# Another bilinear scheme for the first layer of a top-1 expert, with the sums of the second layer's weights on another engine

## The chip, the cores and the metric

The kernel runs on one core of a Trainium2 chip. The metric is the device time of one execution in microseconds (us). The engines are named as in the profile: PE is the matrix engine (PEld its weight loads), DVE, ACT and POOL the vector, scalar and GpSimd engines, SP the one that issues most transfers.

## The reference

An attention block feeds a mixture of experts. Everything is fp32.

```python
def _attn_ref(q, k, v, alpha):                       # 4 x 8 heads, 768 steps, 48 wide
    for t in range(S):
        state = alpha[:, :, t, :, None] * state + np.einsum('bhd,bhe->bhde', k[:, :, t], v[:, :, t])
        y[:, :, t] = np.einsum('bhd,bhde->bhe', q[:, :, t], state)
    ...
def _moe_ref(x, expert_emb, tau, w1, w2):            # x 3072 x 384; 8 experts; w1 384 x 1024, w2 1024 x 384
    xn = x / (np.linalg.norm(x, axis=-1, keepdims=True) + 1e-06)
    ...
    expert_idx = np.argmax(logits, axis=1)
    ...
    gate_w = probs[np.arange(N), expert_idx]
    for e in range(E):
        mask = expert_idx == e
        h = np.maximum(x[mask] @ w1[e], 0.0)
        out[mask] = gate_w[mask, None] * (h @ w2[e])
```

Each of the 3,072 rows goes to one expert, about 384 rows to each; a row's result is its gate times `relu(x w1) w2`.

## The kernel before

From 0 to about 162 us of the profile the kernel computes the attention and the router, and writes the rows to HBM sorted by expert. The rest of the time is the mixture of experts. An expert's rows are taken as three whole blocks of 128 rows, plus a half block of 64 rows that runs only for experts with more than 384 rows. Expert 0 is computed in the plain way (`first_layer`, `second_layer`), two of its blocks early; experts 1 to 7 run as follows (`run(i)`), and the change concerns these.

**First layer** (`first_layer_blocks`). The transposed rows `xT` (384 x 384) and `w1` (384 x 1024) are cut in blocks: `w1` into 2 x 3 blocks of 128 x 512 (`halves_w1`), the rows into 3 x 3 blocks of 128 x 128. The product is made by a bilinear scheme of 15 block products in place of 18. Sums of weight blocks are in `w1_m` (ten of 128x512), sums of row blocks in `xT_m` (16 of 128x128). One product is 4 matmuls of 128 columns each. [...]`bank(j)` names one of four in pool `ps_q` (tiles `pq`), and pools `ps_y` (tiles `pyo`) and `ps_x` (tiles `pxg`) have two each. Several products accumulate in one bank and are read out between two of them; the part read is copied (ACT) or added (DVE) into a block of the hidden rows `hT`, and `relu` runs in place on ACT. A product into a bank waits for the last reader of that bank. The chains start in banks 2, 1, 0 and 3:

```python
            A, B, C, D = (grid(j) for j in (2, 1, 3, 0))
```

**Second layer.** The third block goes through `second_layer` (16 rows in the profile, 128x384). The first two go through `second_layer_pair`, seven products of 2 x 2 blocks, each 4 matmuls of 192 columns, in banks 0, 1 and 3:

```python
            a, b, d = (bank(j)[:, 0:m] for j in (0, 1, 3))
            ...
            product(a, a22, t4, False, True)
            done_pair[:] = pe[0], by_act(nc.scalar.mul, y1[:, 0:m], a, g1)
            done_pair.append(scatter(y1, col[:, 1:2]))
```

Its sums of hidden blocks `s1` to `s4` come from `mix_hidden` (DVE, 128x512), its sums of `w2` blocks `t1` to `t4` from `mix_weights` (DVE, 128x768). The results `y` are scattered to their rows by POOL (`scatter`).

**What sets the order.** PE's products are kept in written order by `pe_turn`: each is issued after the one before. `by_dve` and `by_act` do the same for the DVE and ACT work that they carry. What carries none of these is placed by a scheduler from dependences. `between` transposes a block of the next expert's rows on PE and copies it to `xT` on ACT; `squares` takes the squared norm of a block of its rows on ACT; `norm`, `begin_gates` and `gates_end` make its gates. The sums of the next expert's `w1` blocks (`mix_first_weights`) run on POOL, those of its row blocks (`mix_first_rows`) on DVE beside the second layer. For expert 1 the `w1` sums are on DVE. Weights have three buffers (`NW`), loaded by SP two experts ahead.

**The half block** (`run_extra`) stands behind a branch on a value loaded at run time. In the program it comes after the first matmuls of the next expert's first layer, and every engine passes the branch. It ran for experts 0, 3 and 4.

Of the kernel before, what the change touches and what calls it, by code (L numbers as in the profile page):

```python
# [9 lines left out]
FP32 = mybir.dt.float32  # L10
I32 = mybir.dt.int32
AF = mybir.ActivationFunctionType
# [15 lines left out]
def kernel(  # L28
# [797 lines left out]
    with ExitStack() as c3:  # L826
# [12 lines left out]
        w2_m = wp.tile([P, 4, FT // 2, DM // 2], FP32, name="w2_m")  # L839
        hT_m = xp.tile([P, 4, FT // 2, P], FP32, name="hT_m")  # L840

        w1_m = wp.tile([P, 10, F // 2], FP32, name="w1_m")
        xT_m = xp.tile([P, 16, P], FP32, name="xT_m")
        NG = 3
        gt_s = [xp.tile([P, NC + 1], FP32, name=f"gt{i}") for i in range(NG)]
        sx_s = [xp.tile([P, NC + 1], I32, name=f"sx{i}") for i in range(NG)]
# [139 lines left out]
        def by_dve(call, *args, **kwargs):  # L986
            with turn_of(dve):
                dve[:] = [call(*args, **kwargs)]  # L988
            return dve[0]

        def by_act(call, *args, **kwargs):
            with turn_of(act):
                act[:] = [call(*args, **kwargs)]  # L993
            return act[0]
# [5 lines left out]
            n, m = FT // 2, DM // 2  # L1000
            return [[w2_t[:, i * n : i * n + n, j * m : j * m + m] for j in range(2)] for i in range(2)]

        def mix_weights(w2_t):

            (b11, b12), (b21, b22) = quarters(w2_t)
            t1, t2, t3, t4 = (w2_m[:, k] for k in range(4))
            for to, x, y in ((t1, b12, b11), (t2, b22, t1), (t3, b22, b12), (t4, b21, t2)):
                by_dve(nc.vector.tensor_tensor, to, x, y, ALU.subtract)

        def hidden(hT, t):  # L1010

            return [hT[:, j * FT // 2 : (j + 1) * FT // 2, t * P : (t + 1) * P] for j in range(2)]
# [9 lines left out]
            by_dve(v.tensor_tensor, s2, s1, a11, ALU.subtract)  # L1022
            by_dve(v.tensor_tensor, s4, a12, s2, ALU.subtract)

        def halves_w1(w1_t):

            return [[w1_t[:, k, j * F // 2 : (j + 1) * F // 2] for k in range(KT)] for j in range(2)]

        def mix_first_weights(i, by):

            (a11, a12, a13), (a21, a22, a23) = halves_w1(w1_s[i % NW])
            g, g2, e, f2, q9, q7, q10, k6, q13, k = (w1_m[:, j] for j in range(10))
            for to, x, y, op in (
                (g, a11, a12, ALU.add), (g2, g, a22, ALU.subtract), (e, a12, a13, ALU.subtract),
                (f2, e, a22, ALU.subtract), (q9, a21, g2, ALU.subtract),
                (q7, a23, q9, ALU.subtract), (q10, g, q7, ALU.subtract),
                (k, f2, a23, ALU.add), (k6, k, a21, ALU.subtract),
                (q13, q7, a13, ALU.subtract),
            ):
                by(to, x, y, op)  # L1040

        def mix_first_rows(i):

            xT, m = xT_s[i % 2], xT_m
            b1, b2, b3 = (xT[:, k, 0 : NC * P].rearrange("p (t n) -> p t n", n=P) for k in range(KT))
            y1, z1, y2, z2, x5, x12, x10, x6, x1, x4, x7, x13, s, x15, x11, x14 = (
                m[:, j : j + 1] for j in range(16)
            )
            v = nc.vector

            def one(b, t):
                return b[:, t : t + 1]

            v.tensor_tensor(m[:, 0:2], b2[:, 1:3], b3[:, 1:3], ALU.add)
            v.tensor_tensor(y2, one(b2, 0), one(b1, 0), ALU.subtract)
            v.tensor_tensor(x1, y1, y2, ALU.add)
            v.tensor_tensor(x11, y2, one(b3, 0), ALU.add)
            v.tensor_tensor(m[:, 4:6], b1[:, 0:2], y1.to_broadcast([P, 2, P]), ALU.subtract)
            v.scalar_tensor_tensor(
                out=x4, in0=y2, scalar=-1.0, in1=one(b3, 1), op0=ALU.mult, op1=ALU.subtract  # L1060
            )
            v.tensor_tensor(x7, z1, one(b1, 0), ALU.subtract)
            v.tensor_tensor(s, one(b2, 2), one(b3, 1), ALU.add)
            v.tensor_tensor(m[:, 6:8], s.to_broadcast([P, 2, P]), b1[:, 0:3:2], ALU.subtract)
            v.tensor_tensor(x13, one(b1, 2), z1, ALU.subtract)
            v.tensor_tensor(z2, one(b1, 2), one(b2, 2), ALU.subtract)
            v.tensor_tensor(x14, one(b3, 0), x7, ALU.subtract)
            v.tensor_tensor(x15, one(b1, 1), x6, ALU.add)

        def first_layer_blocks(w1_t, hT, between, squares):  # L1070

            (a11, a12, a13), (a21, a22, a23) = halves_w1(w1_t)
            g, g2, e, f2, q9, q7, q10, k6, q13, k = (w1_m[:, j] for j in range(10))
            y1, z1, y2, z2, x5, x12, x10, x6, x1, x4, x7, x13, _, x15, x11, x14 = (
                xT_m[:, j] for j in range(16)
            )
            (c11, c21), (c12, c22), (c13, c23) = (hidden(hT, t) for t in range(NC))
            n = FT // 2

            def grid(j):  # L1080
                return bank(j)[:, 0 : n * P].rearrange("p (f t) -> p f t", t=P)

            A, B, C, D = (grid(j) for j in (2, 1, 3, 0))

            def product(to, left, right, start, stop):
                with pe_turn():
                    for f in range(n):
                        pe[:] = [nc.tensor.matmul(  # L1088
                            to[:, f], lhsT=left[:, f * P : (f + 1) * P], rhs=right,
                            start=start and f == 0, stop=stop, skip_group_check=True,  # L1090
                        )]

            def add(c, p):
                by_dve(nc.vector.tensor_tensor, c, p, c, ALU.add)

            def relu(c, p):
                return by_act(nc.scalar.activation, c, p, AF.Relu)

            product(A, a22, x1, True, False)
            by_act(nc.scalar.copy, c21, A)  # L1100
            product(B, g2, y1, True, False)
            by_act(nc.scalar.copy, c12, B)
            product(D, a13, x11, True, True)
            by_act(nc.scalar.copy, c11, D)
            between()
            squares()
            product(A, f2, y2, False, False)
            add(c11, A)
            product(B, g, x5, False, False)
            add(c11, B)  # L1110
            relu(c11, c11)
            D = grid(0)
            product(D, a11, x12, True, True)
            add(c12, D)
            between()
            product(A, e, x4, False, False)
            add(c12, A)
            relu(c12, c12)
            squares()
            product(B, q7, x7, False, False)  # L1120
            by_act(nc.scalar.copy, c13, B)
            product(C, q10, x10, True, False)
            by_act(nc.scalar.copy, c23, C)
            between()
            squares()
            squares()
            product(A, k6, x6, False, False)
            add(c13, A)
            product(B, q9, z1, False, False)
            add(c23, B)  # L1130
            product(C, q13, x13, False, True)
            add(c13, C)
            relu(c13, c13)
            product(A, k, z2, False, False)
            add(c23, A)
            relu(c23, c23)
            product(B, a23, x14, False, True)
            add(c21, B)
            relu(c21, c21)
            between()  # L1140
            product(A, a21, x15, False, True)
            return relu(c22, A)

        def second_layer_pair(w2_t, hT, gate, col):

# [74 lines left out]
        def run(i):  # L1220
# [6 lines left out]
            pair = blocks_run(i) == NC  # L1227
            dve[:] = [] if pair else ready
            if pair:
                mix_weights(w2_t)  # L1230
                left, late = list(range(len(nxt))), list(range(len(nxt)))
                if nxt:
                    known = begin_gates(i + 1, by_dve)

                def between():
                    if left:
                        prepare(i + 1, left.pop(0), lambda *args: by_act(nc.scalar.copy, *args))

# [8 lines left out]
                first_layer_blocks(w1_t, hT, between, squares)  # L1247
# [143 lines left out]
```

## Time and profile before

| | us |
|---|---|
| time, median of 3 runs | 408.04 (407.83 to 408.78) |
| the profiled execution's own time | 416.09 |
| its span (first to last instruction) | 414.2 |
| mean granted clock of PE, as a share of full speed | 0.988 |
| mixture of experts | about 162 to 410 of the span |
| one expert (the one that ends at 365.84) | 29.39 |
| of it: first layer; third block's second layer; pair's second layer | 15.09; 5.16; 9.14 |

The profile is of one execution, which was slower than the median of the runs. Its page gives busy time of each engine, the span in slices, and groups of instructions as "line engine op, output<-input, partitions x elements, count | busy us, mean ns of one | idle time before and what ended it". One fp32 matmul of the program shows as two rows of the matrix engine.

### The profile page before, as it was taken

Reading aid. Unit: us, or ns where it says so; the run is one execution under the profiler, and the core shown is the slowest. Engines: PE = TensorE matmul, PEld = TensorE weight load, DVE = VectorE, ACT = ScalarE, POOL = GpSimd, SP = SyncE. Lnnn points to the kernel's source line nnn. Section 1 sums busy time; section 2 is a strip of 40 time slices with the busy share of each in tenths; the row PEclk is TensorE's granted clock in tenths of the full one; section 3 lists DMA queues with packets and bytes.
Section 4 is the critical chain, followed back from the end, with each engine's and each line's share of the span. In section 5 each row is a group of like instructions: output and inputs, shape, how many; then the busy total and the mean of one; then the engine's idle time right before and its main releaser. Section 6 shows DMA issues by size and latency. Waiting matters only on the chain. (4 is left out here: it accounts for less than half of the span.)

```text
span 414.2 us, 12556 instructions
## 1 busy us (share of the span) xinstructions
PE 396.5 (96%) x4954; PEld 353.6 (85%) x4954; DVE 282.9 (68%) x638; ACT 195.2 (47%) x481; POOL 220.8 (53%) x284
## 2 busy tenths in 40 slices
PE   6999999999999789999999999999999999999994
PEld 6889989898899567679989989899979979979974
DVE  7878979698989216872696695691594389397530
ACT  4455545455555324463653734823651572662320
POOL 7455677776666336721853834822761581682001
PEclk8999999999999899999999999999999999999998
DMA  9999999999987892695604706505601900101001
GB/s 137 158 165 154 152 193 181 193 174 189 206 180 172 283 359 102 183 350 181 220 18 160 254 18 223 183 19 183 227 19 41 358 9 19 40 2 41 15 16 44
DMA packets 119379, 60.28 MB, mean 146 GB/s; under 512 B 102287, under 2 KB 113816, under 8 KB 119312
## 3 DMA queue, kind: packets, MB, share of 16 engines
q1 hardware_dynamic: 115208, 49.14, 49.6%
q0 software_dynamic: 3728, 10.16, 6.8%
q8 instruction: 46, 0.75, 0.8%
q14 instruction: 21, 0.17, 0.1%
q10 hardware_dynamic: 376, 0.05, 0.1%
HBM read 49.69 MB, written 11.45 MB: 148 GB/s over the span
## 5 line engine op out<-in xcount | busy, mean ns | idle before, releaser
L858 POOL DMA_INDIRECT out_dram<-y,sx x25 | 24.6, 983 | 102.8 <-DVE y L1167 42.3
L988 DVE TENSOR_TENSOR hT<-pq,hT 128x512 f32<-128x512 f32 x63 | 43.4, 691 | 46.4 <-PE pq L1088 41.9
L1088 PE MATMUL pq<-xT_m,w_m 128*128 128x128 f32 x560 | 67.2, 275 | 0.0
L1088 PEld LDWEIGHTS pq<-xT_m,w_m 128*128 128x128 f32 x560 | 64.8, 192 | 0.3 <-issue 0.3
L512 POOL TENSOR_TENSOR qs<-qc,a 128x512 f32<-128x512 f32 x24 | 30.6, 1275 | 33.5 <-DVE a L508 17.6
L1040 POOL TENSOR_TENSOR w_m<-w_m,w 128x512 f32<-128x512 f32 x30 | 43.2, 1447 | 1.4
L971 PE MATMUL pyo<-w,hT 128*128 128x384 f32 x128 | 42.6, 486 | 0.0
L1088 PE MATMUL pq<-xT_m,w 128*128 128x128 f32 x280 | 38.4, 277 | 0.6
L993 ACT ACTIVATE hT<-hT 128x512 f32<-128x512 f32 x35 | 22.1, 631 | 31.2 <-DVE hT L988 31.2
L1088 PEld LDWEIGHTS pq<-xT_m,w 128*128 128x128 f32 x280 | 34.9, 192 | 2.1 <-issue 1.8
L971 PEld LDWEIGHTS pyo<-w,hT 128*128 128x128 f32 x128 | 23.7, 190 | 14.8
L479 DVE TENSOR_TENSOR_SCAN r<-pa,inr 128x511 f32<-128x511 f32 x24 | 29.2, 1217 | 7.0 <-PE pa L194 4.6
L191 PE MATMUL sc<-qs,kr 64*64 64x128 f32 x768 | 29.3, 273 | 4.5 <-issue 4.5
L311 POOL DMA_INDIRECT xs<-x,dest x24 | 24.2, 1009 | 14.4 <-DVE x L655 9.4
L508 DVE TENSOR_TENSOR_SCAN a<-pa,ini 128x512 f32<-128x512 f32 x24 | 29.3, 1222 | 1.1
L1160 PE MATMUL pq<-w_m,hT_m 128*128 128x192 f32 x168 | 28.4, 326 | 0.0
L191 PEld LDWEIGHTS sc<-qs,kr 64*64 64x64 f32 x768 | 22.3, 133 | 7.0 <-issue 6.5
L1160 PEld LDWEIGHTS pq<-w_m,hT_m 128*128 128x128 f32 x168 | 27.5, 190 | 0.0
L191 PE MATMUL pyx<-sm,vt 128*64 128x128 f32 x384 | 26.3, 279 | 0.0
L191 PEld LDWEIGHTS pyx<-sm,vt 128*64 128x64 f32 x384 | 20.5, 136 | 4.1 <-issue 3.4
L1040 POOL TENSOR_TENSOR w_m<-w 128x512 f32<-128x512 f32 x12 | 15.3, 1276 | 15.9 <-PE pq L1088 15.9
L651 ACT COPY lg<-pyx 128x32 f32<-128x32 f32 x24 | 4.4, 185 | 41.0 <-PE px L191 35.1
(229 smaller groups left out, 910.3 us busy)
## 6 DMA issues: line engine op xcount, KB each, us to landing
w<-in_moe_w_dram SPq DMA_DIRECT2D x16, 1536.0 KB
kt<-in_k_dram SPq DMA_DIRECT2D x24, 192.0 KB
qt<-in_q_dram SPq DMA_DIRECT2D x24, 192.0 KB
vt<-in_v_dram SPq DMA_DIRECT2D x24, 192.0 KB
xg<-xs SPq DMA_DIRECT2D x22, 196.5 KB
at<-in_alpha_dram SPq DMA_DIRECT2D x24, 168.0 KB
xg<-xs SPq DMA_DIRECT2D x8, 98.2 KB
at<-in_alpha_dram SPq DMA_DIRECT2D x24, 22.5 KB
```

The source lines that it names most:

```text
L191: last["pe"] = nc.tensor.matmul(*args, **kwargs)
L311: ins = nc.gpsimd.indirect_dma_start(out=xs, out_offset=bass.IndirectOffsetOnAxis(ap=rows, axis=0), in_=x, in_offset=None, bounds_check=E ...
L479: nc.vector.tensor_tensor_scan(r[:, L - 2 :: -1], pa[:, L - 1 : 0 : -1], inr[:, L - 2 :: -1], 1.0, ALU.mult, ALU.add,)
L508: d["a_scan"] = by_dve = nc.vector.tensor_tensor_scan(a, pa, ini, 0.0, ALU.mult, ALU.add)
L512: by_pool = nc.gpsimd.tensor_tensor(qs.rearrange("p n t -> p (n t)"), d["qc"], a, ALU.mult)
L858: ins = nc.gpsimd.indirect_dma_start(out=out, out_offset=bass.IndirectOffsetOnAxis(ap=col, axis=0), in_=y, in_offset=None, bounds_check=N - 1,
L971: pe[:] = [nc.tensor.matmul(py, lhsT=hT[:, f], rhs=w2_t[:, f], start=(f == 0), stop=(f == FT - 1),)]
L988: dve[:] = [call(*args, **kwargs)]
L993: act[:] = [call(*args, **kwargs)]
L1040: by(to, x, y, op)
L1088: pe[:] = [nc.tensor.matmul(to[:, f], lhsT=left[:, f * P : (f + 1) * P], rhs=right, start=start and f == 0, stop=stop, skip_group_check=Tr ...
L1160: pe[:] = [nc.tensor.matmul(to, lhsT=left[:, f], rhs=right[:, f], start=start and f == 0, stop=stop and f == n - 1, skip_group_check=True,)]
```

## The change

The first layer is cut in another way: `w1` into 3 x 4 blocks of 128 x 256 (`columns_w1`), the rows into 3 x 2 blocks of 128 x 192 (`rows_x`). The scheme has 20 block products in place of the 24 of that cut. One product is 2 matmuls of 192 columns. There are 16 sums of weight blocks (128x256) and 13 of row blocks (128x192). The chains are in banks 0, 1, 2 and 3, two further chains follow in banks 0 and 2, and two products stand `alone` in `ps_y`. The first four products take row blocks as they are, without sums. The sums of `w2` blocks are issued on POOL for experts 2 to 7 and stay on DVE for expert 1.

```diff
-        w1_m = wp.tile([P, 10, F // 2], FP32, name="w1_m")
-        xT_m = xp.tile([P, 16, P], FP32, name="xT_m")
+        TH, FQ = NC * P // 2, F // 4
+        w1_m = wp.tile([P, 16, FQ], FP32, name="w1_m")
+        xT_m = xp.tile([P, 13, TH], FP32, name="xT_m")
...
-        def mix_weights(w2_t):
+        def mix_weights(w2_t, by):
...
-                by_dve(nc.vector.tensor_tensor, to, x, y, ALU.subtract)
+                by(to, x, y, ALU.subtract)
...
+        def columns_w1(w1_t):
+            return [w1_t[:, k, j * FQ : (j + 1) * FQ] for k in range(KT) for j in range(4)]
+        def rows_x(xT):
+            return [xT[:, k, t * TH : (t + 1) * TH] for t in range(2) for k in range(KT)]
...
         def mix_first_weights(i, by):
...
+            w = columns_w1(w1_s[i % NW]) + [sum_w1(j) for j in range(12, 28)]
             for to, x, y, op in (
+                (14, 8, 9, ALU.add), (16, 4, 6, ALU.add), (20, 0, 8, ALU.add),
...
+                by(w[to], w[x], w[y], op)
...
+        def first_layer_blocks(w1_t, xT, hT, between, squares):
...
+            c = [hT[:, 2 * j : 2 * j + 2, t * TH : (t + 1) * TH] for t in range(2) for j in range(4)]
...
+            def alone():
+                return grid(ps_y.tile([P, DM], FP32, name="pyo"))
             def product(to, left, right, start, stop):
                 with pe_turn():
-                    for f in range(n):
+                    for f in range(2):
                         pe[:] = [nc.tensor.matmul(
-                            to[:, f], lhsT=left[:, f * P : (f + 1) * P], rhs=right,
+                            to[:, f], lhsT=w[left][:, f * P : (f + 1) * P], rhs=x[right],
...
-            def add(c, p):
-                by_dve(nc.vector.tensor_tensor, c, p, c, ALU.add)
+            def add(j, p, op=ALU.add):
+                by_dve(nc.vector.tensor_tensor, c[j], c[j], p, op)
...
+            A, G, D, B = (chain(j) for j in (0, 1, 2, 3))
+            product(A, 11, 5, True, False)
+            put(7, A)
+            product(G, 4, 4, True, False)
+            put(4, G)
+            product(D, 20, 5, True, False)
+            add(4, D)
+            product(B, 15, 4, True, False)
+            add(7, B, ALU.subtract)
             between()
+            product(A, 13, 9, False, False)
+            put(6, A, -1.0)
...
+            E3 = chain(0)
+            product(E3, 27, 0, True, False)
+            add(1, E3, ALU.subtract)
+            relu(1)
...
+            y = alone()
+            product(y, 0, 15, True, True)
+            add(4, y)
+            relu(4)
             squares()
...
+            X4 = chain(2)
+            product(X4, 23, 18, True, False)
+            add(2, X4, ALU.subtract)
+            relu(2)
             squares()
+            product(E3, 1, 10, False, True)
+            add(5, E3)
+            relu(5)
+            product(B, 25, 16, False, True)
+            add(3, B)
+            relu(3)
+            product(X4, 22, 6, False, True)
+            add(0, X4)
+            relu(0)
             squares()
             squares()
...
-                mix_weights(w2_t)
+                if i == 1:
+                    mix_weights(w2_t, lambda *args: by_dve(nc.vector.tensor_tensor, *args))
+                else:
+                    mix_weights(w2_t, nc.gpsimd.tensor_tensor)
```

`chain(j)` is `bank(j)` seen as two halves of 192 columns; `put` copies a bank into a block of `hT` on ACT, with a sign; `grid` before gave four parts of 128 columns.

More of the change, by code (lines that the diff above doesn't have):

```diff
@@ L1023, in mix_hidden, with sum_w1, sum_x @@
             by_dve(v.tensor_tensor, s4, a12, s2, ALU.subtract)
-        def halves_w1(w1_t):
-            return [[w1_t[:, k, j * F // 2 : (j + 1) * F // 2] for k in range(KT)] for j in range(2)]
+        def columns_w1(w1_t):
+            return [w1_t[:, k, j * FQ : (j + 1) * FQ] for k in range(KT) for j in range(4)]
+        def rows_x(xT):
+            return [xT[:, k, t * TH : (t + 1) * TH] for t in range(2) for k in range(KT)]
+        def sum_w1(j):
+            return w1_m[:, j - 12]
+        def sum_x(j):
+            return xT_m[:, j - 6]
@@ L1029, in mix_first_weights @@
         def mix_first_weights(i, by):
-            (a11, a12, a13), (a21, a22, a23) = halves_w1(w1_s[i % NW])
-            g, g2, e, f2, q9, q7, q10, k6, q13, k = (w1_m[:, j] for j in range(10))
+            w = columns_w1(w1_s[i % NW]) + [sum_w1(j) for j in range(12, 28)]
             for to, x, y, op in (
[L1034 to L1038, printed above, removed]
+                (14, 8, 9, ALU.add), (16, 4, 6, ALU.add), (20, 0, 8, ALU.add),
+                (15, 3, 7, ALU.subtract), (12, 2, 10, ALU.add), (13, 11, 12, ALU.add),
+                (17, 2, 16, ALU.subtract), (19, 0, 14, ALU.add), (18, 5, 15, ALU.add),
+                (21, 16, 13, ALU.subtract), (24, 5, 13, ALU.subtract), (26, 1, 19, ALU.add),
+                (27, 18, 26, ALU.subtract), (23, 2, 6, ALU.subtract), (25, 7, 24, ALU.subtract),
+                (22, 17, 14, ALU.subtract),
@@ L1039, in mix_first_weights @@
             ):
-                by(to, x, y, op)
+                by(w[to], w[x], w[y], op)
         def mix_first_rows(i):
[L1044 to L1083, printed above, removed]
+            xT, v = xT_s[i % 2], nc.vector
@@ new lines, in mix_first_rows, with minus_sum @@
+            x = rows_x(xT) + [sum_x(j) for j in range(6, 19)]
+            def minus_sum(to, a, b):
+                v.scalar_tensor_tensor(
+                    out=x[to], in0=x[a], scalar=-1.0, in1=x[b], op0=ALU.mult, op1=ALU.subtract
+                )
+            for to, a, b, op in (
+                (8, 3, 4, ALU.add), (6, 0, 2, ALU.subtract), (7, 1, 6, ALU.add),
+                (9, 7, 5, ALU.subtract), (11, 4, 7, ALU.add),
+            ):
+                v.tensor_tensor(x[to], x[a], x[b], op)
@@ new lines, in mix_first_rows, with grid, chain @@
+            minus_sum(13, 0, 5)
+            for to, a, b, op in (
+                (12, 0, 4, ALU.subtract), (14, 2, 5, ALU.add), (18, 1, 4, ALU.add),
+            ):
+                v.tensor_tensor(x[to], x[a], x[b], op)
+            minus_sum(17, 8, 9)
+            for to, a, b, op in (
+                (15, 3, 5, ALU.subtract), (10, 0, 3, ALU.add), (16, 0, 1, ALU.add),
+            ):
+                v.tensor_tensor(x[to], x[a], x[b], op)
+        def first_layer_blocks(w1_t, xT, hT, between, squares):
+            w = columns_w1(w1_t) + [sum_w1(j) for j in range(12, 28)]
+            x = rows_x(xT) + [sum_x(j) for j in range(6, 19)]
+            c = [hT[:, 2 * j : 2 * j + 2, t * TH : (t + 1) * TH] for t in range(2) for j in range(4)]
+            def grid(whole):
+                return whole[:, 0 : 2 * TH].rearrange("p (f t) -> p f t", t=TH)
+            def chain(j):
+                return grid(bank(j))
+            def alone():
+                return grid(ps_y.tile([P, DM], FP32, name="pyo"))
@@ L1096, in relu @@
[L1096 to L1104, printed above, removed]
-            between()
-            squares()
-            product(A, f2, y2, False, False)
-            add(c11, A)
-            product(B, g, x5, False, False)
@@ L1110, in first_layer_blocks, with put, relu @@
[L1110 to L1114, printed above, removed]
+            def put(j, p, sign=1.0):
+                if sign > 0:
+                    by_act(nc.scalar.copy, c[j], p)
+                else:
+                    by_act(nc.scalar.mul, c[j], p, -1.0)
+            def add(j, p, op=ALU.add):
+                by_dve(nc.vector.tensor_tensor, c[j], c[j], p, op)
+            def relu(j):
+                by_act(nc.scalar.activation, c[j], c[j], AF.Relu)
@@ new lines, in first_layer_blocks @@
+            A, G, D, B = (chain(j) for j in (0, 1, 2, 3))
[7 more added lines that the diff above has]
+            add(7, B, ALU.subtract)
+            between()
+            product(A, 13, 9, False, False)
+            put(6, A, -1.0)
+            product(G, 17, 11, False, False)
+            put(0, G, -1.0)
@@ new lines, in first_layer_blocks @@
+            product(D, 19, 13, False, False)
+            put(5, D, -1.0)
+            product(B, 18, 12, False, False)
+            add(5, B, ALU.subtract)
+            between()
+            product(A, 12, 14, False, True)
+            put(3, A, -1.0)
+            put(2, A)
+            product(G, 21, 7, False, False)
+            add(2, G)
+            product(D, 9, 14, False, True)
+            put(1, D)
+            add(0, D, ALU.subtract)
+            product(B, 5, 18, False, False)
+            add(1, B)
@@ new lines, in first_layer_blocks @@
+            between()
+            E3 = chain(0)
+            product(E3, 27, 0, True, False)
+            add(1, E3, ALU.subtract)
+            relu(1)
+            product(G, 2, 17, False, True)
+            add(6, G, ALU.subtract)
+            relu(6)
+            y = alone()
+            product(y, 0, 15, True, True)
+            add(4, y)
+            relu(4)
+            squares()
+            y = alone()
+            product(y, 3, 8, True, True)
+            add(7, y)
+            relu(7)
@@ L1115, in first_layer_blocks @@
             between()
-            product(A, e, x4, False, False)
-            add(c12, A)
-            relu(c12, c12)
+            X4 = chain(2)
+            product(X4, 23, 18, True, False)
+            add(2, X4, ALU.subtract)
+            relu(2)
             squares()
[L1120 to L1124, printed above, removed]
+            product(E3, 1, 10, False, True)
@@ L1125, in first_layer_blocks @@
+            add(5, E3)
[6 more added lines that the diff above has]
+            relu(0)
             squares()
             squares()
[L1127 to L1142, printed above, removed]
         def second_layer_pair(w2_t, hT, gate, col):
@@ L1229, in run @@
             if pair:
-                mix_weights(w2_t)
+                if i == 1:
+                    mix_weights(w2_t, lambda *args: by_dve(nc.vector.tensor_tensor, *args))
+                else:
+                    mix_weights(w2_t, nc.gpsimd.tensor_tensor)
                 left, late = list(range(len(nxt))), list(range(len(nxt)))
@@ L1245, in norm @@
                         gates_norm(known, len(nxt), by_dve, by_act)
-                first_layer_blocks(w1_t, hT, between, squares)
+                first_layer_blocks(w1_t, xT, hT, between, squares)
                 mix_hidden(hT, norm)
```

## The prediction

> **What bounds the kernel now.** I read the page's engine totals first, then its slices, then the window of one expert, then the timeline around the place where one expert's products end and the next one's begin.
>
> ```profile
> PE 396.5 (96%) x4954; PEld 353.6 (85%) x4954; DVE 282.9 (68%) x638; ACT 195.2 (47%) x481; POOL 220.8 (53%) x284
> PE   6999999999999789999999999999999999999994
> 350.75:365.84 15.09, 14.94 (x134) 14.78 (x133) 8.11 (x16) 9.23 (x22) 10.49 (x9) 1.00 0.08 29
> 336.45:365.84 29.39, 29.24 (x206) 26.90 (x205) 21.39 (x45) 15.10 (x33) 16.48 (x14) 1.00 0.06 21
> ```
>
> PE is busy 96% of the span. In the last two lines (start:end, length, busy time of PE, PEld, DVE, ACT and POOL, granted clock) one first layer takes 15.09 us and a whole expert 29.39 us, and PE lacks 0.15 us in each. So DVE's 21.4 and POOL's 16.5 us per expert cost nothing while they come in time: a change counts here by columns streamed through PE and by waits put into PE's queue.
>
> ```profile
> 341.61 2.76 PE L1160 MATMUL pq<-w,hT 128*128 128x192 f32 x16
> 344.21 4.06 PE L1160 MATMUL pq<-w_m,hT_m 128*128 128x192 f32 x24
> 349.41 1.50 PE L1160 MATMUL pq<-w_m,hT 128*128 128x192 f32 x8
> 350.59 0.80 PEld L1088 LDWEIGHTS pq<-xT_m,w 128*128 128x128 f32 x6
> 350.75 1.44 PE L1088 MATMUL pq<-xT_m,w 128*128 128x128 f32 x8
> 350.95 0.42 ACT L993 ACTIVATE y<-pq,gt 128x192 f32<-128x192 f32 x1 [3.52 <-PE pq L1160]
> 351.70 0.30 PEld L1088 LDWEIGHTS pq<-xT_m,w 128*128 128x128 f32 x2 [0.31 <-issue]
> ```
>
> This is the timeline (start, duration, engine, line, operation, count, idle time before it). The second layer's last product begins at 349.41 and its last matmul at 350.59; the next expert's first layer follows at 350.75 without a gap. ACT empties that last product's bank only from 350.95 to 351.37, beside the new products. The only idle PE time is 0.31 us at 351.70, where the instructions ahead of the half-block branch drain.
>
> **What the Trainium skill says.** (1) "TensorE: Matmul & The Clock Gate", § Back-to-back issue gap, gives N/2.4 + 2.5 ns for an isolated warm matmul. With the columns counted twice, my fit for fp32, that is 109.2 ns at 128, 162.5 at 192 and 322.5 at 384. The trace, start to start: 111.7, 162.5 (24 in 3.90 us, 344.21 to 348.11) and 322.6. It agrees at 192 and 384, and 128 costs 2.5 ns more. (2) "PSUM — Partial Sum Buffer", § PSUM bank collisions raise a hardware error, says that the hardware does not arbitrate two engines in one bank, so software must guard by bank. The trace shows the cost of such a guard nowhere at this boundary, since the next product uses another bank. (3) "SBUF — State Buffer", § Who interferes with whom: a DVE instruction with two SBUF inputs contends with a GpSimd instruction that reads SBUF, one with at most one SBUF input does not. The trace agrees: adds of PSUM and SBUF take 691 ns beside POOL's sums, sums of two SBUF operands of that size 680 to 690 alone and 1290 to 1490 beside POOL. (4) "GPSIMD Engine Reference", § 4.1 Engine selection, puts two-input work at about twice DVE's time on GpSimd; here 128x512 takes 1276 on POOL and 680 on DVE.
>
> **The products.** Each fp32 matmul is two rows here. A first layer was 15 products x 4 x 2 = 120 rows of 128 columns; it becomes 20 x 2 x 2 = 80 rows of 192. The streamed columns are the same, 120 x 128 = 80 x 192 = 15,360. Time: 120 x 0.1117 = 13.40 us before, 80 x 0.1625 = 13.00 after, **-0.40 us** for each of seven first layers, all on the path. The four groups of three transposes (0.327 us each) and the branch's drain stay: 13.40 + 1.31 + 0.38 = 15.09, as measured.
>
> **The new wait.** The second layer's pair uses banks 0, 1, 3; its last product (`a22`, `t4`) is in bank 0 and is read by `y1[:, 0:m]` on ACT. Before, the first layer started in bank 2 (`A`), which the pair never touches. Now `A` is bank 0, so its first LDWEIGHTS waits for that ACT instruction, and everything on PE is behind it: the branch, 19 products, the transposes. Priced from the rows: the last matmul at 350.59 is released to ACT at 350.95; ACT takes 0.42, to 351.37; from an evacuation's end to the LDWEIGHTS it frees is 0.06 (DVE ends 188.61, PEld 188.67), the matmul 0.03 later. That is 351.46 instead of 350.75, 0.71 us, and about 0.04 for the cold restart of the weight load: **+0.75 us**. Bounds: 0.42, ACT's own time, if the handovers cost nothing (less than 0 is excluded, since a wait only adds), and 0.95 if the branch is lengthened too. PE's branch loads a value and compares it; by the trace's records that ended at 350.23, beside the last product and 1.4 us ahead of the drain. Now both are queued behind the wait and end 0.9 us after it; the two or three matmuls ahead of the branch drain at 0.9 as well, so I take 0. It happens before six first layers (experts 2 to 7). Expert 1's first layer follows no pair, so has no such wait; before it there is a wait for x and the half block in any case, and DVE's w1 sums for it cost PE some 0.15: I count -0.25 there.
>
> Sum: 6 x (-0.40 + 0.75) - 0.25 = **+1.85 us**. The profiled execution, 416.09 us (414.2 span and 1.9 around it), would become 417.9; the median of 408.04, 2% under that execution, 409.9.
>
> **Inside the first layer.** Sums left in PSUM are now read 14 times by DVE (before 9) and copied 8 times by ACT (before 5), each 128x384. A line through DVE's 128x256 (about 400 ns) and 128x512 (691) gives 0.55 us: 7.7 us of 14.3. ACT: 8 copies at 0.48 (128x384 has that row), 8 relus at about 0.53 (from 631 at 512), 4 copies of xT and 4 squares with their accumulator reads (0.48, 0.73) come to 12.9 of 14.3, though overlapped issue leaves less. A product into a bank waits for its last reader. Walking all 20 with 0.20 us from product end to reader, the tightest is the last one (`X4`, bank 2): it wants `add(2, X4)` at 13.13 and would start at 13.67. At least 0.5 us is spare everywhere, so I cost this at 0; the cover is the three products in other banks between two uses of one. The second layer needs the last relus by 0.8 us less than I find. The squares moved to the end make `s2` on DVE ready about 6 us after the second layer starts; its product needs it at 7.76.
>
> **Sums of x** (13 of 128x192, cadence about 0.27 = 3.5 us, before 3.1) are needed only from the fifth product on, since the first four take x itself. They end some 0.7 us later, ahead of the pair's DVE evacuations, the last of which that PE waits for comes 2 us later: 0. **Sums of w1** on POOL: 16 of 128x256 at 613 ns (row L537) = 9.8 us, before ten at 1276 to 1447 = 13.6. **Sums of w2**, four of 128x768: DVE's 0.956 x 4 = 3.8 us per expert go, but PE waited for none of them, so nothing is gained. On POOL each is 1276 x 768/512 = 1.9 us (estimate), 7.7 in all; per expert POOL then has 9.8 + 7.7 + 3 scatters of 0.98 = 20.5 of 29.4 us. Expert 1's stay on DVE. POOL's queue has them ahead of the pair's scatters (`t1` to `t3` before `y0`, `t4` before `y1`), so these leave 2.4 and 3.4 to 5 us later; the three y buffers are wanted 20 us later, so 0. The w1 sums follow at 7 to 17 us into the first layer (before from 5.4); they are needed in the next one: 0. SP's transfers are the same in number; an expert's weights are issued about 1 us later and are used more than 30 us later: 0. The tail after the last pair does not change.
>
> **Rivals.**
>
> A. *The wait on bank 0 costs nothing* (faster): ACT's emptying is met by something PE waited for anyway. For it: nothing in the profile; against it: PE has no gap at 350.75. Then 7 x -0.40 + 0.15 = -2.65, 405.4 us. It decides the sign at a wait of 0.44 us a boundary; between 0.30 and 0.58 the result is within 0.8 us of no change, which is 0.2%, about what a measurement of this kernel can tell from no change.
>
> B. *The evacuations fall behind* (slower than my forecast): 30 PSUM and relu steps in 13 us, in an order by hand, on ACT above all. It decides when an add or a copy with its handover exceeds the 0.65 us of a product for several in a row. Each first layer then loses 0.3 to 1 us more: +2 to +7, 412 to 417 us. Against it: the 0.5 us of slack.
>
> C. *DVE's adds meet POOL's sums on the shared port*: the operand order is now SBUF first, PSUM second. If ten adds rise from 0.55 to 1.1 us, a first layer loses 3 to 4 us once the slack is used: from 431 on. Against it: 691 ns beside POOL with the same two memories.
>
> D. *The move to POOL does what it is for but not for PE*: DVE has 3.8 us more room in 29.4 and PE, which never waited for those sums, gains 0. This is inside my forecast; were PE to wait for `t3` or `t4` on POOL, 1.9 us x 6 would be lost, 421. `t4` is done over 20 us before its product.
>
> **How the numbers follow.** Forecast with the wait at 0.6 to 0.95: 0.70, 409 to 411.1. Wait only partly felt: 0.10, 408.0 to 408.8. A: 0.07. B: 0.09. C and a late POOL: 0.04. So faster 0.07, same 0.10, slower 0.83. The range 408.0 to 413.5 leaves out A, C and the upper half of B, some 0.16.
>
> **What would show it.** Right: at the boundary PEld idle some 0.7 us before the first layer's first LDWEIGHTS, released by ACT y; a first layer of 14.7 us from its first matmul (80 rows at 162.5); an expert of 29.74 instead of 29.39; DVE's busy time about 10 us less (6 x 3.8, less 7 x 1.5 for more adds and some for the sums of x); POOL rows of 128x768 near 1.9 us. Wrong: no idle time there (A); idle time inside the first layer with DVE or ACT hT as releaser (B); adds of 128x384 over 0.9 us (C); a pair's product released by POOL (D).

## The result, and the profile after

The changed kernel takes 422.03 us (median of 6 runs, 419.93 to 423.66), the kernel before 408.56 in the same comparison: a ratio of **1.0301** (95% interval 1.0265 to 1.0336), slower. The forecast was 409.9 with a range of 408.0 to 413.5. The profiled execution took 420.01 us, with a span of 418.2.

The spans (414.2 and 418.2) are no measure here: the profiled execution of before came some 8 us later to the experts, by a slower stage ahead of them. I compare the stretch from the start of expert 1's pair to the start of expert 7's: 211.80 to 399.25 before, **187.45 us**, and 204.21 to 403.26 after, **199.06 us**: 11.6 more.

First the page's totals, its slices of PE and of the granted clock, then four windows of the changed kernel: a pair, the first layer after it (expert 2), and those of experts 3 and 6.

```profile
PE 393.4 (94%) x4674; PEld 348.5 (83%) x4674; DVE 257.6 (62%) x655; ACT 206.0 (49%) x516; POOL 252.0 (60%) x344
PE   7899999989999899999999969999999996999994
PEclk9999999999999999999999998999999998899999
```

```profile
204.21:213.98 9.77, 9.26 (x57) 8.96 (x55) 5.88 (x21) 2.56 (x7) 5.23 (x4) 1.00 0.05 17
213.98:228.79 14.81, 14.66 (x92) 14.31 (x93) 6.56 (x12) 9.04 (x22) 14.13 (x18) 1.00 0.80 287
244.87:264.11 19.24, 16.34 (x93) 15.92 (x94) 7.01 (x13) 9.05 (x22) 15.08 (x18) 0.91 0.64 218
349.26:369.68 20.42, 17.21 (x93) 16.79 (x93) 7.01 (x13) 9.05 (x22) 13.81 (x17) 0.83 0.06 21
```

The pair of the kernel before, for comparison (its first layer is shown with the prediction):

```profile
341.61:350.75 9.14, 9.14 (x57) 9.07 (x56) 8.41 (x24) 2.01 (x5) 1.05 (x1) 1.00 0.05 19
```

A usual pair and first layer now take 9.77 + 14.81 = 24.58 us, before 9.14 + 15.09 = 24.23: +0.35, as forecast. But two first layers take 19.24 and 20.42, at a granted clock of 0.91 and 0.83. PE has two new holes in its slices. The waits of PE in that stretch (engine, line, what it waited for: us, times, longest) name them: three lines of the changed kernel, then the only line of the kernel before.

```profile
PE pq L1097 <- PEq L1325: 6.1, 2, 3.2
PE pq L1097 <- ACT y L994: 3.1, 6, 0.5
PE pq L1194 <- ACT u L994: 0.9, 1, 0.9
```

```profile
PE pyo L1198 <- issue: 0.7, 2, 0.4
```

The second is the forecast wait on bank 0. The first is PE's own sequencer (PEq in the profile, where PE's branches and semaphores are listed) at line 1325, the branch of the half block. The third stands in the pair of expert 2, which I come to below. The timeline at expert 3:

```profile
242.90 1.46 PE L1194 MATMUL pq<-w_m,hT 128*128 128x192 f32 x8
244.87 1.24 PE L1097 MATMUL pq<-xT,w 128*128 128x192 f32 x6 [0.51 <-ACT y L994]
249.01 0.56 PE L1097 MATMUL pq<-xT,w 128*128 128x192 f32 x2 [2.90 <-PEq L1325]
249.41 2.50 PE L1097 MATMUL pq<-xT,w_m 128*128 128x192 f32 x8
```

PE waits for ACT (to 244.87), starts the first product, and then stands 2.90 us at the branch. The view of a source line gives the branch instruction itself on PE's sequencer (count, least/median/most ns): two lines of the kernel before, the half blocks' branch and the last branch of the program; then the same two of the changed kernel.

```profile
L1288 PEldq COMPARE_BRANCH  x9: 70/313/450, 220.1 to 406.9; - x9
L1301 PEldq COMPARE_BRANCH  x1: 3533/3533/3533, 409.1 to 409.1; - x1
```

```profile
L1325 PEldq COMPARE_BRANCH  x9: 78/318/3799, 214.4 to 411.0; - x9
L1338 PEldq COMPARE_BRANCH  x1: 3474/3474/3474, 413.1 to 413.1; - x1
```

The records behind the third line are 3,550 ns at expert 3's first layer and 3,799 at expert 6's; the others that skip a half block, 318 to 367. The page lists a DMA queue of kind `instruction` that I take for PE's:

```profile
q8 instruction: 44, 0.72, 0.8%
```

These are transfers of 16 KB; between 15 and 130 us, ahead of the branches, there is one for every 255 records of PE instructions on average, which is why I take them for the fetch of PE's program. The trace's records of them: at expert 3 the branch starts at 245.30, a transfer starts at 246.30 and takes 1.27 us, PE goes on at 248.98. The transfer before lies 248 PE instructions back, as the trace has them; at expert 6, 289. At experts 2 and 7, with short branches, it lies 206 and 153 back. A transfer starts 1.0 to 1.1 us after the three short branches too, so that alone marks nothing; the difference is that PE stands until it has come. So theory 1: a branch that skips the half block is long when the instructions that it lands on have not been fetched. Theory 2, the rival: the branch is long because it now stands behind the wait on bank 0.

The 11.6 us, from the windows: two long branches 4.43 + 5.61 (19.24 and 20.42 less 14.81) = 10.0; boundaries and products 5 x 0.35 + 0.19 = 1.9; expert 2's pair 10.92 in place of 9.77 = 1.1; less 1.5 for the two first layers with a half block inside, which were 0.7 us longer each in that execution of before. Against the stretch of before_pad below (185.94), which has no such slow half blocks, the changed kernel's is 13.1 us longer; the medians differ by 13.5.

### The profile page after: what moved, and what is told of

It reads as the page before. It is cut to its first block, busy times and chain, and to the rows that moved or that the text cites. A ratio compares the mean times of both kernels' runs of the same rounds, so it can differ in the third digit from the quotient of the medians.

```text
span 418.2 us, 12132 instructions
## 1 busy us (share of the span) xinstructions
PE 393.4 (94%) x4674; PEld 348.5 (83%) x4674; DVE 257.6 (62%) x655; ACT 206.0 (49%) x516; POOL 252.0 (60%) x344
## 5 line engine op out<-in xcount | busy, mean ns | idle before, releaser
L989 DVE TENSOR_TENSOR hT<-hT,pq 128x384 f32<-128x384 f32 x84 | 45.5, 553 | 62.3 <-PE pq L1097 43.1
L1097 PE MATMUL pq<-xT_m,w_m 128*128 128x192 f32 x252 | 46.4, 331 | 0.0
L1097 PEld LDWEIGHTS pq<-xT_m,w_m 128*128 128x128 f32 x252 | 42.0, 195 | 0.0
L1051 POOL TENSOR_TENSOR w_m<-w,w_m 128x256 f32<-128x256 f32 x42 | 30.1, 729 | 7.7 <-PE pq L1097 6.2
L1051 POOL TENSOR_TENSOR w_m<-w 128x256 f32<-128x256 f32 x36 | 27.6, 774 | 11.9 <-PE pq L1097 7.1
L994 ACT ACTIVATE hT<-hT 128x384 f32<-128x384 f32 x56 | 28.5, 518 | 11.6 <-DVE hT L989 8.9
L1009 POOL TENSOR_TENSOR w_m<-w 128x768 f32<-128x768 f32 x12 | 22.1, 1843 | 18.6 <-PE pq L1194 18.6
L191 PE MATMUL sc<-qs,kr 64*64 64x128 f32 x768 | 26.0, 271 | 1.5 <-issue 1.5
L191 PEld LDWEIGHTS sc<-qs,kr 64*64 64x64 f32 x768 | 21.0, 133 | 2.0 <-issue 1.9
L1009 POOL TENSOR_TENSOR w_m<-w,w_m 128x768 f32<-128x768 f32 x12 | 21.8, 1819 | 0.6
```

Of the source, the lines that this page charges most:

```text
L191: last["pe"] = nc.tensor.matmul(*args, **kwargs)
L1009: by(to, x, y, ALU.subtract)
L1051: by(w[to], w[x], w[y], op)
L1097: pe[:] = [nc.tensor.matmul(to[:, f], lhsT=w[left][:, f * P : (f + 1) * P], rhs=x[right], start=start and f == 0, stop=stop, skip_group_ch ...
```

## The experiments

The ratio is each kernel's to the kernel before on the same chip. "Stretch" is the 187.45 and 199.06 us from above. "Long" lists the experts ahead of whose first layer PE's branch took over 2 us in the profile.

| kernel | ratio (95%) | stretch | bank waits | long |
|---|---|---|---|---|
| changed | 1.0301 (1.0265-1.0336) | 199.06 | 6 | 3, 6 |
| after_pad | 1.0191 (1.0092-1.029) | 193.12 | 6 | 2 |
| after_warm2 | 1.0187 (1.0139-1.0236) | 193.12 | 6 | 3 |
| after_pad9 | 1.0164 (1.0113-1.0215) | 189.93 | 6 | none |
| after_banks | 0.9968 (0.9938-0.9998) | 185.37 | 0 | 3, 6 (mostly hidden) |
| after_banks_pad | 1.0063 (1.0034-1.0092) | 184.11 | 0 | 3 (mostly hidden) |
| after_banks_pad5 | 0.9974 (0.9949-0.9998) | 185.18 | 0 | 3 (mostly hidden) |
| after_banks_w2dve | 0.9957 (0.9937-0.9978) | 184.84 | 0 | none |
| the same again | 0.9910 (0.9875-0.9944) | 183.44 | 0 | none |
| before_pad | 1.0016 (0.9986-1.0045) | 185.94 | 0 | none |
| before_bank0 | 1.0106 (1.0072-1.0139) | 191.10 | 6 | none |
| before_bank0_pad | 1.0119 (1.0056-1.0182) | 195.42 | 6 | 6 |
| before_w2pool | 0.9987 (0.9967-1.0007) | 186.26 | 0 | none |

**Moving the branch in PE's program, nothing else** (after_pad; the tiny matmuls follow PE's warm-up at 1.5 us):

```diff
             for _ in range(n):
                 mm(pw, lhsT=ident, rhs=ident, start=True, stop=True)
+            for _ in range(16):
+                mm(pw[:, 0:8], lhsT=ident, rhs=ident[:, 0:8], start=True, stop=True)
```

> The changed kernel with 16 tiny matmuls (64 PE instructions, 8 columns each) added to PE's warm-up at the very start; nothing else differs. Theory 1 (instruction fetch): the two half-block branches that took 3.55 and 3.80 us on PE (others 0.36) landed on instructions that were not fetched yet, because of where these branches lie in PE's program (instruction 238 and 255 of a stretch of 256, by my count). Shifted by 64, no branch lies there: both long branches vanish, with the slow matmuls after them; 413 to 415 us instead of 422.0. Theory 2 (the new bank wait makes the branch late, and that is what makes it long): nothing changes for the branches, 422 to 424 us.

The branches at experts 3 and 6 fell to 341 and 339 ns, and that at expert 2 rose to 3,467. Another was long, behind the last pair, at 3,618. So the length goes with the place in the program, as theory 1 has it, and not with the wait, which is there at all six. That the place matters through instructions not yet fetched is still an inference. My count of the bad places was wrong: with two long branches left, and the first real product at 8.28 us where it was at 4.70, the ratio is 1.0191 where I expected some 1.011 to 1.016.

**The same shift on the kernel before** (before_pad, 5 of these matmuls):

> The kernel before with 5 tiny matmuls (20 PE instructions) added to the warm-up at the start. By my count this moves the branch ahead of expert 2's first layer from instruction 227 of its stretch to 247, among those that were long in the changed kernel, and no other. Theory 1: that one branch takes about 3.5 us, of which 1.4 lie beside the pair's last product; with slow matmuls after it +2 to +3 us: 410.5 to 411.5. Theory 2: no wait, no long branch: within 0.5 us of 408.3.

A miss: no branch became long (356 ns at expert 2). In this trace the last transfer came 68 instructions ahead of that branch, in the kernel before 35. So the place must be counted from the last transfer; I had counted it from the start of the program, and by the right count this branch was in no danger.

**Another bank for the first product** (after_banks):

```diff
-            A, G, D, B = (chain(j) for j in (0, 1, 2, 3))
+            A, G, D, B = (chain(j) for j in (2, 1, 0, 3))
...
-            E3 = chain(0)
+            E3 = chain(2)
...
-            X4 = chain(2)
+            X4 = chain(0)
```

> The changed kernel with banks 0 and 2 exchanged in the first layer, so that its first product is again in bank 2, which the pair never touches. The place of the branches in PE's program stays within a few instructions. Theory 1: the wait of 0.64 us at six boundaries goes (-3.8); the two long branches stay, but now begin beside the pair's last product, which hides about 1.4 us of each; 414 to 416.5 us. Theory 2: no wait ahead of the branch, so no long branch either: 409 to 411 us.

```profile
203.18:212.28 9.10, 9.10 (x57) 9.10 (x56) 5.88 (x21) 2.14 (x6) 4.56 (x3) 1.00 0.06 20
212.28:226.99 14.71, 14.56 (x95) 14.21 (x93) 7.01 (x13) 9.46 (x23) 14.04 (x17) 1.00 0.80 288
241.80:257.41 15.61, 14.56 (x94) 14.21 (x93) 7.01 (x13) 9.46 (x23) 14.95 (x18) 1.00 0.74 268
```

The windows are a pair, expert 2's first layer and expert 3's. The pair is 9.10 without the wait, and the first layer 14.71. The branches at experts 3 and 6 are still 3.30 and 2.98 us long, which speaks against theory 2; but they start beside the pair's last product, so that only 0.90 (15.61 - 14.71) and 0.71 us of them show. The ratio fell by 0.033, more than I expected (13.6 us in place of 6 to 8): a long branch is cheap where PE has work queued ahead of it, and costs nearly its whole length, and slow matmuls after it, where a wait has emptied the queue. The wait on bank 0 did harm twice.

**Both edits** (after_banks_pad, 16 tiny matmuls; after_banks_pad5, 5 of 32 x 8):

> Both edits: banks 0 and 2 exchanged, and 64 PE instructions added at the start. Theory 1: neither bank waits nor long branches are left. If what my prediction said of the products holds (-0.37 us in each first layer), this is 405 to 407 us; if the rest of the change costs something that I have not seen yet, 409 to 411. Theory 2: the same as with the banks alone.

> The changed kernel with banks 0 and 2 exchanged and 5 tiny matmuls (20 PE instructions) at the start. With the banks alone two branches still took 3.30 and 2.98 us, of which 0.90 and 0.71 showed in the first layers. Moved by 20 instructions they should find the next stretch fetched or on its way. Theory 1: both short or hidden, 1.2 to 1.8 us less than with the banks alone, less about 0.5 for the tiny matmuls: a ratio of 0.990 to 0.995 to the kernel before. Rival: the branches cost nothing while they lie beside the pair's last product: 0.9968 as with the banks alone.

The first has a stretch 1.3 us shorter than with the banks alone, but a ratio of 1.0063. The tiny matmuls delay the start (the first real product begins at 8.29 us, before at 4.71). In the profiled execution the first pair came 2.0 us later than with the banks alone, and the tail, from the start of the last pair to the end, was 1.3 us longer; two branches stand there, 3.68 and 2.31 us. The second cleared expert 6's branch (441 ns) but not expert 3's (3,077); its ratio tells it from the kernel with the banks alone in neither direction. Both fall short of my expectation: shifting is no way to tune, since each shift moves all branches.

**The bank wait alone, in the kernel before** (before_bank0):

```diff
-            A, B, C, D = (grid(j) for j in (2, 1, 3, 0))
+            A, B, C, D = (grid(j) for j in (0, 1, 3, 2))
...
-            D = grid(0)
+            D = grid(2)
```

> The kernel before with banks 0 and 2 exchanged in its first layer of 15 products: the first product now stands in bank 0, which ACT still reads for the pair's last result. Nothing else changes. Theory 1: a wait of about 0.78 us (as the changed kernel showed: the pair 9.77 us instead of 9.10, and 0.10 more in the first layer) at six boundaries, +4.7 us: a ratio of 1.0105 to 1.0125. The branches stay short. Rival: the wait belongs to the new scheme, which has its first product's operands later: no wait here, ratio 1.00.

As expected, and PE's waits show it with the old products:

```profile
PE pq L1088 <- ACT y L993: 3.1, 6, 0.5
PE pq L1088 <- PEq L1288: 0.5, 1, 0.5
```

The second line is a branch of 450 ns ahead of expert 2's first layer: behind the wait even a short one showed once.

**The long branch too, in the kernel before** (before_bank0_pad; 25 tiny matmuls of 32 x 8):

> The same with 25 tiny matmuls (100 PE instructions) at the start of the kernel, so that by my count the branches ahead of the first layers of experts 3 and 6 are reached some 250 instructions after PE's last instruction fetch, ahead of the next one. If both causes that I name are the whole of the slowdown, the 15-product kernel now loses as much as the changed one: +4.7 for six waits, +4 to 5.6 for each long branch behind such a wait, up to 1.5 for the tiny matmuls: a ratio of 1.030 to 1.040. If the long branches come from the new scheme, the ratio stays at 1.011 to 1.015.

```profile
351.70 0.94 PE L1090 MATMUL pq<-xT_m,w 128*128 128x128 f32 x6 [0.51 <-ACT y L995]
355.81 0.77 PE L1090 MATMUL pq<-xT_m,w 128*128 128x128 f32 x2 [3.17 <-PEq L1290]
```

One of the two branches that I aimed at became long (3,523 ns, 248 instructions after the last fetch); at expert 3 a fetch came 49 instructions ahead, and it stayed at 426. The 15-product kernel then stands 3.17 us at expert 6, as the changed one did. The stretch grew by 4.3 us against before_bank0, and the profiled execution by 3.4 (421.68 against 418.25; the tail is 0.6 us shorter, the start 0.4 earlier). So a long branch behind such a wait needs no new scheme. The ratio does not show it: 1.0119 lies where I had put the rival, from four executions of 417.19 to 421.68 us, of which the longest is the profiled one. Whether the branch was long in the other three is not known.

**Two more shifts of the changed kernel** (after_warm2: `warm(7)` to `warm(2)`; after_pad9: 9 tiny matmuls of 32 x 8):

> The changed kernel, banks and all, with 2 warm-up matmuls at the very start instead of 7: PE's program is 20 instructions shorter ahead of the branches, nothing else differs. The bank wait stays at six boundaries. If the branches ahead of experts 3 and 6 are now short (an instruction fetch ahead of them), the two losses of 4.4 and 5.6 us go, and what is left is what my prediction counted (+0.35 us a boundary) and DVE's wait for x: a ratio of 1.002 to 1.008. Each branch that stays long adds 0.011 to 0.014. Rival: the rest of the slowdown has another cause too: over 1.012 with short branches.

> The same question from the other side: the changed kernel with 9 tiny matmuls (36 PE instructions) more at the start. 1.003 to 1.010 if no branch is long, 0.011 to 0.014 more for each that is.

after_warm2 lost one long branch of two, and its ratio fits the one that is left. after_pad9 has none; yet its ratio is above what I gave for that, and above the 1.012 that I had set as the sign of a further cause. Its PE waits:

```profile
PE pq L1099 <- ACT y L996: 3.1, 6, 0.5
PE pq L1099 <- issue: 1.5, 1, 1.5
```

The 1.5 us stand at expert 2, two products behind the branch, where no engine releases PE and the transfer of the next instructions had started only at 222.62, 1.1 us after the branch. I take it for the same cause; no run separates it. The tiny matmuls at the start were counted at nothing too. The stretch, 4.0 us over before_pad's, makes 1.0% of the 1.64%; the rest is open.

**The sums of w2** (before_w2pool has the second part of the change alone; after_banks_w2dve has the first part alone, with the banks exchanged):

```diff
-                if i == 1:
+                if i >= 1:
                     mix_weights(w2_t, lambda *args: by_dve(nc.vector.tensor_tensor, *args))
```

> The kernel before with the second part of the change alone: the sums of w2 on POOL for experts 2 to 7, the first layer of 15 products as it was. My prediction: worth nothing, ratio 0.998 to 1.002, as PE waited for none of these sums; POOL then has 13.6 + 7.7 us of sums and 3 of scatters in 29.4 us. Rival: POOL, with 24 of 29.4 us, delays the sums of w1 or a pair's product: 1.005 or more.

> The changed kernel with banks 0 and 2 exchanged, and the sums of w2 on DVE for all experts, as before the change. It takes the second part of the change alone away. My prediction: it is worth nothing, since PE never waited for these sums: within 0.5 us of the kernel with the banks alone (ratio 0.9956 to 0.998). Rival 1: DVE needs the room, now that it has 14 adds in a first layer: slower by 1 us or more. Rival 2: POOL's 7.3 us of sums delay something that PE waits for: faster by 1 us or more.

The ratios show no effect: 0.9987 (0.9967 to 1.0007) on the old first layer; on the new one 0.9957 beside 0.9968, with intervals that overlap. But there the move also took the long branches away (PE's program has 220 semaphore records in place of 232, so its branches lie elsewhere):

```profile
L1325 PEldq COMPARE_BRANCH  x9: 70/318/431, 220.1 to 404.3; - x9
```

The traces show one more thing. With the sums on DVE, DVE's first gate instruction for the next expert (`gtop`) comes right behind the last of them (222.07 us in after_banks_w2dve). With the sums on POOL it stands at the end of the first layer (228.75 in after_banks, 230.58 in the changed kernel). There it waited for the next expert's rows, 1.5 to 2.4 us in each of the seven kernels with the new first layer and these sums on POOL, and one of their pairs took 0.3 to 1.2 us longer than the others (9.65 in place of 9.10 in after_banks). after_banks_w2dve and its repetition have neither, and with the old first layer (before_w2pool, 232.69) it waited for nothing.

**The fastest version once more** (the same program):

> The version that came out fastest, once more: the new first layer with banks 0 and 2 exchanged and the sums of w2 on DVE for all experts. It had a ratio of 0.9957 (0.9937 to 0.9978) and no long branch. What I count for it: -0.38 us in each of seven first layers, no bank wait: -2.7 us, 0.9935; the same program again should give 0.993 to 0.998. If it is not below 1, the gain was the chip's scatter.

0.991 (0.9875 to 0.9944), more than I expected: it is faster than the kernel before in both comparisons, by under 1%. Seven times -0.38 us is -2.7, 0.9935.

## Why the prediction was wrong

**Products: right.** -0.40 us was forecast; 15.09 became 14.71 where no wait precedes it (-0.38). The number comes from 192-column rows at 162.5 ns, which the pair showed.

**The wait on bank 0: right, in place and price.** 0.75 us forecast; the pair grew from 9.14 to 9.77 and the first layer lost 0.10 in restarting: 0.73. Put into the old kernel alone it made it slower by 1.06%, 4.3 us.

**The branch: the step that failed.** Branch and drain "end 0.9 us after it; the two or three matmuls ahead of the branch drain at 0.9 as well, so I take 0", with 0.95 as the upper bound of the wait. I sized the branch by its record at that boundary, 337 ns and hidden (the nine of that line are 70 to 450), though another branch of the same kind stood in the same trace at 3,533 ns, at the end of the program. I saw that the branch had been hidden and now was queued behind the wait, named it, and then bounded it by the case that had been hidden. The missing term measured 4.43 + 5.61 us. It came from two things together: the new product list moved two branches to places in PE's program where they are long (by my reading, because the instructions that they land on are not fetched), and the wait left nothing in PE's queue to cover them. No size of that was to be had from the diff; a bound of 0 to 3.5 us a branch was, and with it the range would have reached beyond 420. The sign came out for the reason given, +0.35 us a boundary, but that reason makes some 2 of the 13.5 us.

**"At least 0.5 us is spare everywhere": nearly.** DVE's first gate instruction now stands ahead of the last adds, put there by the move of the w2 sums (see the experiments), and waited once for the next rows (expert 2):

```profile
230.58 0.18 DVE L989 TENSOR_REDUCE gtop<-xg 128x4 f32<-128x32 f32 x1 [2.34 <-DMA xg<-xs]
```

The pair behind it took 1.1 us more, where the working had 0.5 us spare. The rest held: adds at 0.55 us forecast and 554 ns measured, none lengthened beside POOL, so rivals B and C did not happen.

```profile
L989 DVE TENSOR_TENSOR hT<-hT,pq x72: 540/554/556, 216.7 to 398.3; 128x384 f32<-128x384 f32 x72
L1051 POOL TENSOR_TENSOR w_m<-w,w_m x35: 720/728/739, 220.7 to 369.3; 128x256 f32<-128x256 f32 x35
L1009 POOL TENSOR_TENSOR w_m<-w,w_m x12: 1805/1815/1834, 211.5 to 386.9; 128x768 f32<-128x768 f32 x12
```

POOL's sums of w1 took 728 ns, not the 613 of the row I used (another operation's), those of w2 1.8 us where 1.9 were estimated; POOL is not on the path, so neither counted. DVE's busy time fell by 25.3 us (282.9 to 257.6) where I forecast some 10: I had not counted that POOL's shorter sums of w1 are over when DVE's sums of hidden blocks run, so that 14 of these took 682 ns each in place of 1,288. That was off PE's path too. One reading was loose: the 0.31 us at 351.70 are idle time of the weight loads; PE itself lacks 0.15. **Sums of w2:** right that nothing is gained, but not that nothing is lost; they cost the wait for rows above. **Rival A** is out: the wait showed at all six boundaries. What I counted for expert 1's first layer (-0.25) was not measured by itself.

**What stays open.** Which branch is long was not predicted reliably in any of these kernels. Counting the half blocks' branches that skip, over all fourteen traces: all nine with 242 to 319 PE instructions since the last transfer began took 2.6 to 3.8 us; all 43 with 29 to 193 took 0.31 to 0.45; of 15 with 195 to 226 two were long; three with 10 to 16, where a transfer had begun 0.7 to 1.9 us before, took 0.5 to 1.7. The count alone does not decide, so the fetch fits these figures but is not shown to be the cause. What starts a transfer, I can't say. Padding that leaves all branches short and costs nothing was not found.

## What to carry to other kernels

At a seam between two stages of an engine that never rests, look at which bank the first product writes and who still reads it: two bank numbers exchanged in a list were worth 3.3% here, more than the scheme around them. Before an instruction that is hidden is moved behind a wait, give it its longest record in the trace as a bound, not the median of its covered ones. Where code stands behind branches, compare versions by a stretch of the trace between two marks and read the branches' own records, since any edit moves where they fall. And work that leaves an engine moves what stood behind it there: look at what that will wait for in its new place.

## What the runs showed of the hardware that was not expected

A branch on PE that skips a half block (230 to 253 records of PE instructions where it runs) took 0.31 to 0.45 us in 56 of 70 records and 2.6 to 3.8 us in 11; DVE, ACT and POOL take 37 to 69 ns for the same branch. In the changed kernel a transfer of 16 KB begins 1.0 us after each of the two long branches and lasts 1.3 to 1.4, and PE goes on 1.4 to 1.6 us after it has ended.

After such a stop the granted clock was lower for a while. In all fourteen traces there are five stops of PE of 2.9 to 3.2 us at a branch. At each the clock record goes to 0.5, from 2.4 to 5.1 us after the branch began, and stays there for 3.4 us (6.8 at expert 6 of the changed kernel); from the first pair to the last it does so nowhere else, and not after the stop of 1.5 us in after_pad9. Some matmuls of 192 columns show 527 ns there in place of 326, and the changed kernel's two first layers lost 1.5 and 2.4 us more than the stop itself.
